# Moving the memsets of two V tiles behind the first scores, and three epsilon additions from GpSimd to VectorE, in a fused attention and GLU kernel

## The chip, the cores and the metric

The kernel runs on one core of one Trainium2 chip. The metric is the device time of one execution in microseconds (us), lower is better. The profile gives a second length, the span: from the first to the last instruction in the trace. Time and span are not the same thing.

PE is TensorE, PEld its weight loads, DVE is VectorE, ACT is ScalarE, POOL is GpSimd.

## The reference

```python
x  = A_x                                   # [1, 2048, 512], bf16
xn = layernorm(x)                          # (x - mean) / sqrt(var + 1e-5)
# A: sliding-window attention, 32 heads of 16, window 256
q, k, v = split_heads(xn @ wqkv)
p  = softmax(where(mask, q @ k.T * 16**-0.5, -1e9))
A  = merge_heads(p @ v) @ wo
# B: bilinear GLU
B  = ((xn @ w_gate) * (xn @ w_up)) @ w_down    # 1792 hidden
return x + A + B
```

## The kernel before

The 2048 rows are 16 row tiles of 128, in four chunks of four. PE does the projections, the scores, the values and the GLU in one hand-made order. Before PE can start on real work, the four row tiles of the first chunk must be normalised: VectorE makes the statistics, an epsilon is added, GpSimd takes the power -0.5, VectorE applies it (`xn`), PE transposes `xn`, ScalarE copies the transpose, and PE projects V, then K and Q.

```python
def setup(self):
    ...
    for _ in range(38):                                   # warm-up of PE
        nc.tensor.matmul(wps[:], lhsT=ident[:], rhs=ident[:], start=True, stop=True)
    ...
    self.new_values()                                     # first V tile

def new_values(self):                                     # three memsets on GpSimd
    ...
    nc.gpsimd.memset(self.heads(V)[:, :, :, 16:18], 1.0)
    nc.gpsimd.memset(V[:, VW - 16:], 0.0)
    nc.gpsimd.memset(VS[:, SW - 16:], 0.0)

def norm_scale(self, t, n=4):
    ...
    (nc.gpsimd if t else nc.vector).tensor_scalar(out=ve[:], in0=mv[:, :, 1], scalar1=1e-5, ...)   # var + eps
    nc.gpsimd.tensor_tensor(out=rs[:], in0=ve[:], in1=self.mhalf[:, 0:n], op=ALU.pow)

def first_chunk(self):
    self.new_chunk(0)
    for b in range(2):
        self.norm_stats(b, 1)
        self.norm_scale(b, 1)
    for b in (0, 1, 2, 3):
        self.norm_apply(b)                                # xn of tile b, on VectorE
        if b < 2:
            self.norm_stats(b + 2, 1)
            self.norm_scale(b + 2, 1)
    self.norm_transpose(0, False)
    for b in range(4):
        if b < 3:
            self.norm_transpose(b + 1, False)             # PE, then a copy on ScalarE
        self.proj_v(b, engine="act")                      # PE, then a copy on ScalarE
    self.proj_qk(0, 0, 1, engine="dve")                   # "first K projection" below
    self.proj_qk(0, 0, 0, engine="act")
    self.swap_halves(0, self.nc.scalar)
    for _ in range(2):
        self.new_values()                                 # second and third V tile
    self.proj_qk(0, 1, 1, engine="dve")
```

The softmax here doesn't subtract the row's maximum and nothing guards it: scores larger than these inputs give would overflow.

Of the kernel before, what the change touches and what calls it, by code (L numbers as in the profile page):

```python
# [11 lines left out]
ALU = mybir.AluOpType  # L12
# [16 lines left out]
class Kernel:  # L29
# [133 lines left out]
    def norm_scale(self, t, n=4):  # L163

        nc = self.nc
        mv = self.stats[t][0]
        ve = self.small.tile([128, n], F32, tag="ve", name="ve")
        (nc.gpsimd if t else nc.vector).tensor_scalar(out=ve[:], in0=mv[:, :, 1], scalar1=1e-5, scalar2=None,
                                                      op0=ALU.add)
        rs = self.small.tile([128, n], F32, tag="rs", name="rs")  # L170
        nc.gpsimd.tensor_tensor(out=rs[:], in0=ve[:], in1=self.mhalf[:, 0:n], op=ALU.pow)
        for u in range(t, t + n):
            self.stats[u][2] = rs
# [75 lines left out]
# [7 lines that stand above are left out]
            self.norm_apply(b)  # L256
# [6 lines that stand above are left out]
                self.norm_transpose(b + 1, False)  # L263
            self.proj_v(b, engine="act")
        self.proj_qk(0, 0, 1, engine="dve")
        self.proj_qk(0, 0, 0, engine="act")
        self.swap_halves(0, self.nc.scalar)
        for _ in range(2):
            self.new_values()
        self.proj_qk(0, 1, 1, engine="dve")  # L270


# [247 lines left out]
    def run(self):  # L520
        self.xns, self.stats, self.sums = {}, {}, {}
        self.now, self.free = 0, dict(act=0, dve=0)
        self.setup()
        NCH, LAG = self.NCH, 2
        RESERVE = 36
        self.first_chunk()
        steps, self.first, self.last = [], {}, {}
        for T in range(NCH):
            for pieces in self.batches(T):
                for c, *_ in pieces:  # L530
                    self.first.setdefault((T, c), len(steps))
                    self.last[T, c] = len(steps)
                steps.append((T, pieces))
        due = {g: key for key, g in self.last.items()}
        self.beside = {}
        work = self.fillers()
        total = sum(w[0] for w in work) - RESERVE + SCORES * len(steps) + VALUES * (len(due) - 1)
        spent, n = 0, 0
        self.free = dict(act=0, dve=0)
        valued, ready = -1, -1  # L540

        def fill(upto, group):
            nonlocal spent, n
            while n < len(work):
                cost, f, before, after = work[n]
                if after is not None and after > valued:
                    break
                if spent + cost / 2 > upto and not any(
                        w[2] is not None and w[2] <= group for w in work[n:]):
                    break  # L550
                spent += cost
                self.now = spent
                f()
                n += 1

        def values(g):
            nonlocal spent
            if g not in due:
                return False
            spent += VALUES  # L560
            self.now = spent
            self.values(*due[g])
            return True

        def divide(g):
            nonlocal ready
            self.divide(*due[g])
            ready = g

        for g, s in enumerate(steps):  # L570
            fill(-1, g)
            valued = ready
            spent += SCORES
            self.now = spent
            self.scores(*s)
            upto = total * (g + 1) / len(steps)
            if values(g - LAG):
                fill(min(spent + 4, upto), g)
                divide(g - LAG)
            for _, f in self.beside.get(g, ()):  # L580
                f()
            if g < len(steps) - 1:
                fill(upto, g)
                self.mask_diag(*s)
        T = NCH - 1
        self.ps_s.__exit__(None, None, None)
        late = self.ctx.enter_context(self.tc.tile_pool(name="ps_late", bufs=1, space=bass.MemoryType.PSUM))
        self.late = [late.tile([128, 512], F32, tag=f"L{i}", name=f"L{i}") for i in range(4)]
        fill(spent + 10, -1)
        self.mask_diag(*steps[-1])  # L590
        fill(spent + 10, -1)
        self.values(*due[len(steps) - 1], self.late)
        spent += VALUES
        divide(len(steps) - 1)
        valued = ready
        fill(spent + 15, -1)
        for b in range(3):
            self.wo(T, b, (3,))
            self.store(T, b)
        fill(10 ** 9, -1)  # L600
        assert n == len(work)
        self.wo(T, 3, (0, 1, 2, 3))
        self.store(T, 3, 0)
        self.store(T, 3, 1, True)
# [37 lines left out]
```

## Time and profile before

| | before |
|---|---|
| time, median | 267.34 us (267.24 to 268.01) |
| span of the profiled execution | 265.6 us |
| PE busy | 257.5 us, 97% |
| first K projection on PE | 11.12 us |

The page of the kernel before: its length, the busy time of each engine, and by engine the chain of work that ended last.

```profile
span 265.6 us, 8876 instructions
...
PE 257.5 (97%) x3860; PEld 119.0 (45%) x3881; DVE 176.1 (66%) x339; ACT 176.4 (66%) x143; POOL 114.6 (43%) x278
...
PE 94%; DVE 2%; issue 1%; DMA 1%; POOL 0%
```

PE is the limit nearly everywhere. The exception is the head, the first 11 us. Here is the timeline of the head of the kernel before. The columns are start (us), duration (us), engine, line, operation, output and inputs, shape, and in brackets the idle time of the engine before it and what ended it.

```profile
3.64 0.18 DVE L159 BATCH_NORM_AGGREGATE mv<-st 128x2 f32<-128x6 f32 x1
3.86 0.15 DVE L168 TENSOR_SCALAR ve<-mv 128x1 f32<-128x1 f32 x1
3.93 0.69 DVE L158 BATCH_NORM_STATS2 st<-x 128x6 f32<-128x512 bf16 x1
...
5.77 0.18 DVE L159 BATCH_NORM_AGGREGATE mv<-st 128x2 f32<-128x6 f32 x1
5.91 0.41 DVE L179 TENSOR_SCALAR xn<-x,mv,rs 128x512 bf16<-128x512 bf16 x1
...
6.37 0.40 PE L198 MATMUL xTp<-ident,xn 128*128 128x128 bf16 x4 [0.29 <-DVE xn L179]
...
7.08 0.41 DVE L179 TENSOR_SCALAR xn<-x,mv,rs 128x512 bf16<-128x512 bf16 x1
7.22 0.35 POOL L168 TENSOR_SCALAR ve<-mv 128x1 f32<-128x1 f32 x1 [0.18 <-DVE mv L159]
7.55 0.40 PE L198 MATMUL xTp<-ident,xn 128*128 128x128 bf16 x4
...
8.18 0.33 POOL L127 MEMSET V<- 128x256 bf16 x1
...
8.27 0.83 DVE L179 TENSOR_SCALAR xn<-x,mv,rs 128x512 bf16<-128x512 bf16 x1 [0.77 <-POOL rs L171]
...
8.85 0.60 ACT L218 ACTIVATE V<-vp 128x512 bf16<-128x512 f32 x1
9.16 0.40 PE L198 MATMUL xTp<-ident,xn 128*128 128x128 bf16 x4 [0.34 <-DVE xn L179]
...
9.59 0.60 ACT L199 ACTIVATE xnT<-xTp 128x512 bf16<-128x512 bf16 x1
...
11.12 2.54 PE L239 MATMUL qkp<-xnT,Wqkv 128*128 128x512 bf16 x11
```

Three things are to be seen. The last `xn` (8.27 us) takes 0.83 us while GpSimd does memsets; the others take 0.38 to 0.41. PE waits for that `xn` before the last four transposes (9.16 us). And an epsilon addition costs VectorE little by itself: it starts 0.22 us after the aggregate of its tile, and the next instruction follows 0.07 us later (3.64, 3.86, 3.93).

### The profile page before, as it was taken

To read this page: it belongs to the slowest core of one execution; us is meant where nothing else is said; L and a number is where in the kernel's file an instruction comes from. 1 tells how busy PE (TensorE), PEld (TensorE's weight loads), DVE (VectorE), ACT (ScalarE), POOL (GpSimd) and SP (SyncE) were. 2 spreads that over 40 slices of the span, in tenths; PEclk is the share of its full clock that TensorE was granted. 3 is DMA by queue.
4 is the path that set the end of the run, shared out by engine and by line. 5 is a ranking of instruction groups with operands and counts; after the bars stand their busy time and mean duration, and the time that the engine had idled before them with its cause. 6 is when DMAs were issued, how large, how long until landed. Compare 5 with 4: busy or idle time off the path is not lost.

```text
span 265.6 us, 8876 instructions
## 1 busy us (share of the span) xinstructions
PE 257.5 (97%) x3860; PEld 119.0 (45%) x3881; DVE 176.1 (66%) x339; ACT 176.4 (66%) x143; POOL 114.6 (43%) x278
## 2 busy tenths in 40 slices
PE   7999999999999999999999999999999999999994
PEld 7444444444444444444444444444444444444453
DVE  5477898787757667667765866766652676867152
ACT  3667687788556678687755667678866566767500
POOL 6324342426574535334585443435444353344500
PEclk9999999999999999999999999999999999999999
DMA  6999911120151000002022100000200010000002
GB/s 199 373 353 340 265 23 22 23 48 2 20 86 37 22 2 0 4 2 47 2 59 63 42 2 2 0 4 6 45 2 20 25 40 2 2 0 6 0 2 80
DMA packets 19351, 15.12 MB, mean 57 GB/s; under 512 B 7280, under 2 KB 19312, under 8 KB 19312
## 3 DMA queue, kind: packets, MB, share of 16 engines
q1 hardware_dynamic: 18624, 14.23, 18.8%
q8 instruction: 30, 0.49, 0.8%
q10 hardware_dynamic: 688, 0.33, 0.5%
q14 instruction: 9, 0.07, 0.1%
HBM read 9.70 MB, written 2.10 MB: 44 GB/s over the span
## 4 chain that ended last, share of the span: by engine, by line
PE 94%; DVE 2%; issue 1%; DMA 1%; POOL 0%
PE up L390 19%; PE gp L379 19%; PE psd L410 16%; PE qkp L239 11%; PE S L294 10%; PE acc L348 7%; PE psd L416 5%; PE vp L227 5%; PE L L410 2%; DVE st L158 1%; DMA x<-in_A_x_dram 1%; PE L L416 1%; DVE xn L179 1%; PE L L348 0%; DVE mv L159 0%
## 5 line engine op out<-in xcount | busy, mean ns | idle before, releaser
L301 ACT ACTIVATE P<-S 128x2048 bf16<-128x2048 f32 x75 | 140.7, 1876 | 47.4 <-PE S L294 39.2
L147 POOL TENSOR_SCALAR_AFFINE_SELECT P<-P 64x256 bf16<-64x256 bf16 x224 | 98.6, 440 | 128.9 <-ACT P L301 117.9
L390 PE MATMUL up<-xnT,Wu 128*128 128x512 bf16 x224 | 60.0, 380 | 0.0
L379 PE MATMUL gp<-xnT,Wg 128*128 128x512 bf16 x224 | 58.9, 380 | 0.0
L394 DVE TENSOR_TENSOR hT<-up,gsb 128x512 bf16<-128x512 f32 x56 | 38.5, 687 | 19.5 <-PE up L390 18.0
L410 PE MATMUL psd<-Wd,hT 128*128 128x512 bf16 (+1 forms) x195 | 48.9, 368 | 1.9 <-issue 1.8
L325 DVE TENSOR_TENSOR P<-P,diag 128x512 bf16<-128x512 bf16 (+1 forms) x75 | 29.9, 399 | 9.8 <-ACT P L301 9.8
L410 PEld LDWEIGHTS <-hT 128*128 128x128 bf16 x238 | 21.2, 98 | 25.0 <-issue 2.7
L354 DVE STREAM_TRANSPOSE at<-acc 128x512 f32<-128x512 f32 x30 | 19.7, 696 | 18.8 <-PE acc L348 18.8
L379 PEld LDWEIGHTS <-Wg 128*128 128x128 bf16 x224 | 20.7, 98 | 25.6 <-issue 1.9
L294 PE MATMUL S<-Q,K 16*64 16x320 bf16 (+4 forms) x720 | 30.9, 260 | 0.1
L390 PEld LDWEIGHTS <-Wu 128*128 128x128 bf16 x224 | 19.9, 98 | 25.0 <-issue 3.3
L294 PE MATMUL S<-Q,Ko 32*64 32x320 bf16 (+4 forms) x720 | 31.0, 260 | 0.0
L218 ACT ACTIVATE gsb<-gp 128x512 bf16<-128x512 f32 x34 | 20.0, 596 | 15.5 <-PE gp L379 13.5
L239 PE MATMUL qkp<-xnT,Wqkv 128*128 128x512 bf16 x128 | 30.0, 380 | 0.0
L294 PEld LDWEIGHTS <-K 16*64 16x64 bf16 x720 | 12.1, 103 | 31.8 <-issue 31.4
L348 PE MATMUL acc<-P,VS 64*32 64x320 bf16 (+4 forms) x672 | 18.7, 254 | 0.0
L348 PE MATMUL acc<-P,V 64*32 64x320 bf16 (+4 forms) x672 | 18.5, 254 | 0.0
L239 PEld LDWEIGHTS <-Wqkv 128*128 128x128 bf16 x128 | 11.7, 98 | 14.6 <-issue 1.6
L220 DVE CAST gsb<-gp 128x512 bf16<-128x512 f32 x22 | 15.2, 691 | 3.4 <-PE gp L379 2.0
L416 PE MATMUL psd<-Wo,OT 128*128 128x512 bf16 (+1 forms) x59 | 16.2, 369 | 0.2 <-issue 0.2
L348 PEld LDWEIGHTS <-V 64*32 64x32 bf16 x720 | 14.5, 90 | 3.2 <-issue 2.6
(56 smaller groups left out, 195.5 us busy)
## 6 DMA issues: line engine op xcount, KB each, us to landing
out_dram<-y SPq DMA_DIRECT2D x15, 128.0 KB, 1.7
Wg<-in_B_w_gate_dram SPq DMA_DIRECT2D x2, 896.0 KB, 10.9
Wu<-in_B_w_up_dram SPq DMA_DIRECT2D x2, 896.0 KB, 12.4
Wd<-in_B_w_down_dram SPq DMA_DIRECT2D x1, 1792.0 KB, 17.3
Wqkv<-in_A_wqkv_dram SPq DMA_DIRECT2D x3, 512.0 KB, 5.8
x<-in_A_x_dram SPq DMA_DIRECT2D x1, 1024.0 KB, 10.8
VS<-V SPq DMA_DIRECT2D x6, 144.0 KB, 2.8
x<-in_A_x_dram SPq DMA_DIRECT2D x1, 512.0 KB, 11.0
```

The costliest lines, as they stand in the source:

```text
L147: nc.gpsimd.affine_select(out=v, in_=v, pattern=pattern + [[1 if diag else -1, 64]], compare_op=ALU.is_ge if diag else ALU.is_gt, fill=0.0 ...
L218: nc.scalar.activation(out=out, in_=in_, func=ACT.Copy)
L239: nc.tensor.matmul(ps[:], lhsT=self.Wqkv[:, k, lo:lo + 128], rhs=self.xnT[T][:, :, k, :], start=(k == 0), stop=(k == 3))
L294: nc.tensor.matmul(S[64 * par:64 * par + 64, e, col:col + n], lhsT=(self.Ko if par else self.K)[U][rows, c, keys], rhs=self.Q[T][rows, c, ...
L301: nc.scalar.activation(out=P[:, :, 0:col], in_=S[:, :, 0:col], func=ACT.Exp, scale=0.25)
L325: self.nc.vector.tensor_tensor(out=v, in0=v, op=ALU.min, in1=self.diag.unsqueeze(1).unsqueeze(1).to_broadcast([128, 4, n, 64]))
L348: nc.tensor.matmul(accs[par][32 * e:32 * e + 32, q:q + n], lhsT=v, rhs=P[rows, e, col:col + n], start=(i == 0), stop=(i == len(todo) - 1), ...
L379: nc.tensor.matmul(ps[:], lhsT=self.Wg[:, k, 128 * f:128 * f + 128], rhs=self.xnT[T][:, :, k, :], start=(k == 0), stop=(k == 3))
L390: nc.tensor.matmul(ps[:], lhsT=self.Wu[:, k, 128 * f:128 * f + 128], rhs=self.xnT[T][:, :, k, :], start=(k == 0), stop=(k == 3))
L394: nc.vector.tensor_tensor(out=self.hT[T][:, f, :], in0=ps[:], in1=self.gsb[:], op=ALU.mult)
L410: nc.tensor.matmul(ps, lhsT=self.hT[T][:, f, 128 * b:128 * b + 128], rhs=self.Wd[:, f, c0:c1], start=(f == 0), stop=False)
L416: self.nc.tensor.matmul(ps, lhsT=self.OT[T][:, c, 128 * b:128 * b + 128], rhs=self.Wo[:, c, c0:c1], start=False, stop=(c == 3))
```

## The change

The intent: get the memsets of the second and third V tile out of the way of the last `xn`, and save the first chunk's norms a hand-over from VectorE to GpSimd by adding epsilon where the variance is made.

```diff
@@ norm_scale
-        (nc.gpsimd if t else nc.vector).tensor_scalar(out=ve[:], in0=mv[:, :, 1], scalar1=1e-5, scalar2=None,
-                                                      op0=ALU.add)
+        (nc.vector if t < 4 else nc.gpsimd).tensor_scalar(out=ve[:], in0=mv[:, :, 1], scalar1=1e-5, scalar2=None,
+                                                          op0=ALU.add)
@@ first_chunk
         self.swap_halves(0, self.nc.scalar)
-        for _ in range(2):
-            self.new_values()
         self.proj_qk(0, 1, 1, engine="dve")
@@ run, in the loop over score groups g
             self.scores(*s)
             upto = total * (g + 1) / len(steps)
+            if g in (1, 2):
+                self.new_values()
             if values(g - LAG):
```

## The prediction

> **What bounds the kernel.** TensorE: the page has PE busy 257.5 of 265.6 us (97%) at clock 0.998; the chain of waits is 94% PE. Only in the head, before PE runs without gaps at about 11 us, is something else the limit: the norms of the first chunk's four row tiles, a loop between VectorE and GpSimd. The change acts there. The most it could win is what PE waits there for xn of tiles 1, 2 and 3: 0.29, some 0.25 and 0.34 us (timeline and waits).
>
> **Removed.** (a) Six GpSimd memsets, 8.18 to 8.96 us, beside which the last xn took 0.83 us on VectorE; its siblings took 0.38 to 0.41. The Trainium skill, "SBUF — State Buffer", section "Who interferes with whom", says that VectorE in a two-port mode and GpSimd exclude each other for a whole instruction; the trace agrees. (b) Three epsilon additions on GpSimd (0.29, 0.36, 0.35 us).
>
> **Added.** Three epsilon additions on VectorE. Tile 0 already has one: it starts 0.22 us after its aggregate, the next instruction 0.07 later. Without one, the next instruction follows the aggregate after 0.10 to 0.14. So each adds 0.15 to 0.19 us to VectorE, which is in order and has no slack (its xn waited at most 0.05 us for tiles 1 and 2); the addition for tile b+1 stands in front of xn of tile b.
>
> **The sum (us, before to after).**
> - xn 0: 4.75 to 4.94, hidden: PE warms up until 5.34.
> - xn 1: 5.91 to 6.24; transposes 1 from 6.37 to 6.70.
> - xn 2: 7.08 to 7.58; transposes 2 from 7.55 to 8.04, second V projection from 7.79 to 8.28.
> - xn 3: 8.27 to 8.35..8.55, now 0.41 long, ending at 8.8..8.95, not 9.10. But PE is in the second V projection until 9.14, so transposes 3 go from 9.16 to 9.14: nothing won.
> - ScalarE is in order: the copy of the second V projection (8.85 to 9.34) stands before the copy of transposes 3 (9.59; copies follow at 0.49 at best, so 9.83). The fourth V projection needs it: 10.25 to 10.48. First K projection: 11.12 to 11.35.
>
> What the last tile wins, the second and third lose; the head ends level to 0.3 us later, my estimate 0.15 to 0.2.
>
> **Moved.** The memsets come after the masks of the second and third score groups, about 20.6 and 24.7 us. GpSimd idles 2.2 us before the third group; V1 is not needed before about 50 us. The later ones delay the epsilon and power of the next chunk's first tile (24.74) by 0.5 us, towards its xn at 26.20; VectorE has 0.43 us idle soon after. No PE cost expected. PE is dense to the end, so a shift of the head passes on one to one.
>
> **Time.** 267.45 us, 8 in 10 between 266.9 and 267.95; the spread of before (267.24 to 268.01) exceeds the effect. Faster by over 2%: 1%; within: 98%; slower: 1%.
>
> **Would show it right:** last xn near 0.41 us; xn 1 and 2 start 0.3 and 0.5 us later; transposes 3 wait for PE, not xn; their copy follows directly on the copy of V; first K projection at 11.2 to 11.4; memsets at 20 to 25 us without a PE gap. **Wrong:** first K projection before 11.0, or transposes 1 and 2 unmoved.
>
> **What would make it wrong.** VectorE may take the short addition in a gap that it has anyway: the head then wins up to 0.3 us. The powers on GpSimd, now starting during an xn, may be held until it ends; if xn 3 comes after 9.1, the head loses more. A memset that blocks VectorE at 25 us could open a PE gap.

## The result, and the profile after

| | before | changed |
|---|---|---|
| time, median of 6 | 267.35 us (267.24 to 268.01) | 267.91 us (267.87 to 269.46) |
| ratio, with 95% interval | | 1.0027 (1.0004 to 1.0051) |

A ratio is the mean time of one kernel's runs over that of the other's of the same rounds, so not quite the ratio of the medians. Five executions of the changed kernel lie between 267.87 and 268.03 us; one took 269.46 us, and that one left the profile. The median lies just inside the predicted range (top 267.95 us); the mean, 268.18 us, lies outside; and the change of the median, 0.56 us, is some five times the 0.11 us that the predicted 267.45 us meant.

The page of the changed kernel, from the 269.46 us execution:

```profile
span 267.4 us, 8874 instructions
...
PE 259.1 (97%) x3860; PEld 119.9 (45%) x3881; DVE 176.2 (66%) x342; ACT 176.3 (66%) x143; POOL 113.8 (43%) x275
```

Since that execution is not typical, I ran the same file again (`after_again` below). Its trace, of 267.86 us with a span of 265.8 us, answers to the head shown before. The same timeline of the typical execution:

```profile
4.59 0.18 DVE L159 BATCH_NORM_AGGREGATE mv<-st 128x2 f32<-128x6 f32 x1
4.80 0.15 DVE L168 TENSOR_SCALAR ve<-mv 128x1 f32<-128x1 f32 x1
4.88 0.40 DVE L179 TENSOR_SCALAR xn<-x,mv,rs 128x512 bf16<-128x512 bf16 x1
...
5.92 0.18 DVE L159 BATCH_NORM_AGGREGATE mv<-st 128x2 f32<-128x6 f32 x1
6.13 0.15 DVE L168 TENSOR_SCALAR ve<-mv 128x1 f32<-128x1 f32 x1
6.21 0.41 DVE L179 TENSOR_SCALAR xn<-x,mv,rs 128x512 bf16<-128x512 bf16 x1
...
6.67 0.40 PE L198 MATMUL xTp<-ident,xn 128*128 128x128 bf16 x4 [0.77 <-DVE xn L179]
...
7.16 1.02 PE L227 MATMUL vp<-Wqkv,xnT 128*128 128x512 bf16 x4
...
7.46 0.15 DVE L168 TENSOR_SCALAR ve<-mv 128x1 f32<-128x1 f32 x1
7.54 0.40 DVE L179 TENSOR_SCALAR xn<-x,mv,rs 128x512 bf16<-128x512 bf16 x1
...
8.02 0.39 PE L198 MATMUL xTp<-ident,xn 128*128 128x128 bf16 x4
...
8.38 0.41 DVE L179 TENSOR_SCALAR xn<-x,mv,rs 128x512 bf16<-128x512 bf16 x1 [0.44 <-POOL rs L171]
...
9.10 0.39 PE L198 MATMUL xTp<-ident,xn 128*128 128x128 bf16 x4
9.30 0.60 ACT L218 ACTIVATE V<-vp 128x512 bf16<-128x512 f32 x1
...
9.79 0.59 ACT L199 ACTIVATE xnT<-xTp 128x512 bf16<-128x512 bf16 x1
...
11.32 2.32 PE L239 MATMUL qkp<-xnT,Wqkv 128*128 128x512 bf16 x10
```

The last `xn` is down to 0.41 us, as intended, and no longer waited for by PE. But `xn` of tiles 1 and 2 start 0.30 and 0.46 us later than before (6.21 and 7.54 against 5.91 and 7.08), because each waits behind epsilon additions that VectorE did not have: two by tile 1, three by tile 2. The first K projection is 0.20 us later (11.32 against 11.12). The moved memsets, in the same trace:

```profile
20.83 0.33 POOL L127 MEMSET V<- 128x256 bf16 x1
...
24.87 0.33 POOL L127 MEMSET V<- 128x256 bf16 x1
```

The slow execution has the same VectorE times (its `xn` start at 5.01, 6.34, 7.67 and 8.51 us; x landed some 0.14 us later than in the typical trace). What differs is PE. The PE lines of its timeline:

```profile
6.80 0.61 PE L198 MATMUL xTp<-ident,xn 128*128 128x128 bf16 x4 [0.72 <-DVE xn L179]
7.20 1.49 PE L227 MATMUL vp<-Wqkv,xnT 128*128 128x512 bf16 x3
...
8.91 0.63 PE L198 MATMUL xTp<-ident,xn 128*128 128x128 bf16 x4 [0.22 <-issue]
...
10.72 0.39 PE L198 MATMUL xTp<-ident,xn 128*128 128x128 bf16 x4
...
12.93 0.59 PE L239 MATMUL qkp<-xnT,Wqkv 128*128 128x512 bf16 x2
```

Three V matmuls (of four; one record is missing) take 1.49 us here, four take 1.02 us in the typical trace. A single one of these matmuls is listed with 0.63 us in the slow trace and 0.38 us in the typical one, so they follow each other at (1.49 - 0.63) / 2 = 0.43 us instead of (1.02 - 0.38) / 3 = 0.21 us: PE ran at half its rate there, until about 10.4 us. The granted clock on the page doesn't show it (it reads 9 in all 40 slices of both traces), because its record begins only when full rate is first granted. That moment can be read from the record: 6.37 us after the start of the span in the trace of before, 5.58 us in the typical trace, 10.37 us in the slow one.

So there are two things to explain: why the typical execution is 0.5 us longer when its span is only 0.2 us longer (265.6 to 265.8), and why some executions lose 1.6 us more (I call these the slow ones).

### The profile page after: what moved, and what is told of

Same layout as the page of the kernel before. It is cut to its first block, busy times and chain, and to the rows that moved or that the text cites. A ratio compares the mean times of both kernels' runs of the same rounds, so it can differ in the third digit from the quotient of the medians.

```text
span 267.4 us, 8874 instructions
## 1 busy us (share of the span) xinstructions
PE 259.1 (97%) x3860; PEld 119.9 (45%) x3881; DVE 176.2 (66%) x342; ACT 176.3 (66%) x143; POOL 113.8 (43%) x275
## 4 chain that ended last, share of the span: by engine, by line
PE 95%; DVE 2%; issue 1%; DMA 1%; ACT 0%
PE up L388 19%; PE gp L377 19%; PE psd L408 16%; PE qkp L239 11%; PE S L292 10%; PE acc L346 7%; PE vp L227 5%; PE psd L414 5%; PE L L408 2%; DMA x<-in_A_x_dram 1%; DVE st L158 1%; PE L L414 1%; PE L L346 0%; PE xTp L198 0%; DVE xn L179 0%
## 5 line engine op out<-in xcount | busy, mean ns | idle before, releaser
L239 PEld LDWEIGHTS <-Wqkv 128*128 128x128 bf16 x128 | 11.7, 98 | 14.6 <-issue 1.6
L227 PE MATMUL vp<-Wqkv,xnT 128*128 128x512 bf16 x60 | 16.3, 403 | 0.2
## 6 DMA issues: line engine op xcount, KB each, us to landing
x<-in_A_x_dram SPq DMA_DIRECT2D x1, 1024.0 KB, 11.7
```

The source lines that it names most:

```text
L227: nc.tensor.matmul(ps[:], lhsT=self.xnT[T][:, b, k, :], rhs=self.Wqkv[:, k, 1024:1536], start=(k == 0), stop=(k == 3))
L239: nc.tensor.matmul(ps[:], lhsT=self.Wqkv[:, k, lo:lo + 128], rhs=self.xnT[T][:, :, k, :], start=(k == 0), stop=(k == 3))
```

## The experiments

All with five rounds, each call on one chip with the kernel before beside it. The median of before was 267.37, 267.34 and 267.34 us, with no execution above 267.47.

### First call: which half of the change, and is it PE's rate?

My first theory (G) was that PE's half rate explains all of it, more of it in one execution and less in another. The rival (V) was that only VectorE's order counts.

**after_again**: no edit.

> The changed kernel again, for a second trace. Theory G (PE rate): the longer PE wait before the transposes of tile 1 (0.72 us instead of 0.29) leaves PE at half rate, one 512-column matmul per 0.43 us instead of 0.216, for longer; how long varies between executions. Then the times spread: about 267.9 us, some near 269.5; a trace of a 267.9 us execution shows fewer or no half-rate V projections, and the first K projection near 11.7 instead of 12.93 us. Theory V (VectorE order alone): every execution pays 0.2 us, the 269.46 us one was an outlier for some other reason.

Measured: 267.86 us median, five executions from 267.85 to 267.97; ratio 1.0020 (1.0006 to 1.0034). No execution near 269.5. The typical loss is stable at 0.5 us, and its trace shows PE at full rate from 5.58 us. First K projection at 11.32, not 11.7. Theory G fails as the cause of the typical loss.

**memset_only**: the memsets alone.

```diff
-        (nc.vector if t < 4 else nc.gpsimd).tensor_scalar(   # as changed
+        (nc.gpsimd if t else nc.vector).tensor_scalar(       # as before
```

> Memsets moved, epsilons of tiles 1 to 3 back on GpSimd. V and G alike: xn 1 and xn 2 start at 5.91 and 7.08 as before, the last xn starts near 8.27 and takes 0.41 us instead of 0.83, first K projection at about 10.85 instead of 11.12, time 267.1 us (0.25 less than before). Theory M (the moved memsets cost time at 22 to 27 us, or where their tiles lie does): 267.5 us or more although the head is shorter.

Measured: 267.15 us median (267.10 to 267.50), 0.22 below before. The last `xn` in its timeline:

```profile
8.28 0.41 DVE L179 TENSOR_SCALAR xn<-x,mv,rs 128x512 bf16<-128x512 bf16 x1 [0.76 <-POOL rs L171]
...
8.83 0.39 PE L198 MATMUL xTp<-ident,xn 128*128 128x128 bf16 x4
...
11.05 2.54 PE L239 MATMUL qkp<-xnT,Wqkv 128*128 128x512 bf16 x11
```

So the memsets do what they were moved for, and no cost shows where they went: in this execution the span is 0.07 us shorter than in the trace of before (265.51 against 265.58), and the first K projection 0.07 us earlier. At 11.05 it came later than the 10.85 expected; in this execution full rate was granted only at 6.96 us, so its first transposes of tile 1 ran at half rate.

**eps_only**: the epsilons alone.

```diff
-        (nc.gpsimd if t else nc.vector).tensor_scalar(
+        (nc.vector if t < 4 else nc.gpsimd).tensor_scalar(   # memsets stay in first_chunk
```

> Epsilons on VectorE, memsets left in place. V: transposes 1 near 6.75, transposes 2 near 8.1, last xn 0.83 us again and ending near 9.35, first K projection 11.3 to 11.5, time 267.6. G: the PE wait before transposes 1 is the same 0.72 us as in the changed kernel, so half-rate matmuls as there: 267.9 to 268.2 us with some executions near 269.5.

Measured: 267.92 us median (267.84 to 267.98), none near 269.5. Its timeline has the early delay and the slow last `xn` together:

```profile
6.65 0.57 PE L198 MATMUL xTp<-ident,xn 128*128 128x128 bf16 x4 [0.58 <-DVE xn L179]
...
8.36 0.83 DVE L179 TENSOR_SCALAR xn<-x,mv,rs 128x512 bf16<-128x512 bf16 x1 [0.44 <-POOL rs L171]
```

The whole loss comes from the epsilons; with them on VectorE, moving the memsets is worth nothing (267.92 without, 267.86 with), since PE is then the limit at the last transposes.

**after_filled**: PE kept busy between the transposes of tiles 0 and 1.

```diff
         self.norm_transpose(0, False)
+        fps = self.s_tiles.tile([128, 4, 512], F32, tag="S", name="fps")
+        for _ in range(8):
+            self.nc.tensor.matmul(fps[:, 0, 0:128], lhsT=self.ident[:], rhs=self.ident[:], start=True, stop=True)
```

> The changed kernel with eight 128-column matmuls of the identity between the transposes of tile 0 and tile 1, so that PE doesn't idle there; VectorE, GpSimd and ScalarE unchanged. G: the V projections run at 0.216 us per matmul in every execution, first K projection at about 11.3 us, time 267.3 to 267.6 us, no execution near 269.5. V: nothing changes, 267.9 us.

Measured: 267.87 us median (267.79 to 268.11), as the changed kernel. A miss for G, and it agrees with `after_again`: idle PE is not what the typical execution pays for. (In its traced execution, the slowest of the five, the first V projection also waited 0.20 us for its weights to land.)

Put together, with the spans that each execution lists (to 0.1 us) beside its time; I call "time less span" the tail:

| | time, median | span, median | tail, mean |
|---|---|---|---|
| before (9 executions) | 267.37 | 265.6 | 1.73 |
| memsets moved | 267.15 | 265.4 | 1.72 |
| epsilons on VectorE | 267.92 | 265.8 | 2.07 |
| both (after_again) | 267.86 | 265.8 | 2.07 |

This table is the turning point. The span moves by 0.2 us, as the head does. The other 0.3 us (1.73 to 2.07) is outside the span, in the tail, and it goes with the epsilons.

### Second call: what lengthens the tail?

Theory C: the tail goes with how many instructions VectorE has. The VectorE rows in the traces, waits included, are 437 before, 437 with the memsets moved, and 439 in both kernels with the epsilons on VectorE. Rival: it comes with the later head or with GpSimd's fewer instructions.

**before_v3**: the kernel before with three idle-time VectorE instructions.

```diff
+        spare = const.tile([128, 1], F32, name="spare")
+        for _ in range(3):
+            nc.vector.memset(spare[:], 0.0)
         self.mhalf = const.tile([128, 4], F32, name="mhalf")
```

> The kernel before with three more VectorE instructions of one column each in its setup, where VectorE waits for x anyway; nothing else. The runs so far left 0.3 us of the 0.5 outside the span: time less span is 1.77 us before, 1.73 with the memsets alone moved, 2.07 and 2.08 with the epsilons on VectorE. Theory C (it goes with the number of VectorE instructions of the program): span 265.6, time less span about 2.07, time 267.65 us. Rival (it comes from the three fewer GpSimd instructions, or from the head being later): span 265.6 and time 267.35, as before.

Measured: 267.75 us median, span 265.7, tail 2.08 with 440 VectorE rows. The head didn't move (first K projection 11.06 us) and GpSimd is untouched. The tail came without a later head and without a change on GpSimd: theory C holds, the rival falls.

**after_vless**: the changed kernel with three setup instructions taken off VectorE.

```diff
-        nc.vector.memset(warm[:], 0.0)
+        nc.gpsimd.memset(warm[:], 0.0)                       # after the identity is made
-        nc.vector.tensor_scalar(out=podd[:], in0=pi[:], ...)
-        nc.vector.tensor_copy(out=self.odd[:], in_=podd[:])
+        self.parity()          # the same mask by six small GpSimd instructions after the norms
```

A first form of this kernel, with the bit operations simply given to GpSimd, was refused by the build (that engine has no such operations).

> The changed kernel with three setup instructions of VectorE (a memset and the two that make the odd mask) made on GpSimd instead, so that VectorE has as many instructions as before. Theory C: span 265.8 as the changed kernel, time less span back at 1.75, time 267.55 us. Rival (head later, or which engine adds epsilon): time less span 2.07 and 267.87 us.

Measured: 267.52 us median, span 265.8, tail 1.72 with 437 rows. The tail is back although the head is as late as in the changed kernel. One of its six executions took 269.20 us; it is the profiled one, with full rate granted at 10.69 us, a second slow trace of the same kind as the first. (Its span and tail, 267.5 and 1.7 us, show that the slow executions lose their time inside the span.)

**after_v1dve**: tests the prediction's ScalarE step.

```diff
-            self.proj_v(b, engine="act")
+            self.proj_v(b, engine="dve" if b == 1 else "act")
```

> The changed kernel with the copy of the second V projection on VectorE instead of ScalarE. The prediction had said that the ScalarE queue (this copy ahead of the copy of transposes 3) holds the fourth V projection by 0.23 us. If so: the copy of transposes 3 starts near 9.5 instead of 9.79 us, first K projection near 11.08 instead of 11.32, span 265.55, time 267.6 (tail 2.07 kept). Rival (PE or xn is the limit, the ScalarE order hides behind it): first K projection at 11.3, span 265.8, time 267.85.

Measured: 267.74 us median (267.68 to 267.83), span 265.7, tail 2.06. It is 0.40 us above before, the changed kernel 0.49 (267.86 less 267.37): about 0.1 us won, less than half of the 0.25 expected. In its timeline the copy of transposes 3 no longer stands behind a V copy:

```profile
9.43 0.69 DVE L220 CAST V<-vp 128x512 bf16<-128x512 f32 x1 [0.61 <-PE vp L227]
...
9.65 0.60 ACT L199 ACTIVATE xnT<-xTp 128x512 bf16<-128x512 bf16 x1 [0.16 <-PE xTp L198]
```

So taking the copy off ScalarE gained something, but less than expected. What ScalarE's order alone costs is not shown, since the edit also gives VectorE a copy of 0.69 us. The traced execution is the slowest of the five, with full rate only from 7.46 us, so its first K projection (11.29) can't be compared closely.

**memset_v1dve**: the same edit on top of memset_only.

> The memsets moved, the epsilons on GpSimd as before, the copy of the second V projection on VectorE: a candidate that beats both. First K projection near 10.87 instead of 11.05, span 265.35, time 267.0 us; if one more VectorE instruction is enough to lengthen the tail, 267.3.

Measured: 267.23 us median (267.13 to 267.67), span 265.3, tail 1.93 with 438 rows. The span is the shortest so far, and one VectorE instruction more took 0.2 us of it back in the tail. In all five executions the tail lies between 1.89 and 1.97, so 438 rows cost a little over half of what 439 cost (0.20 against 0.34 us).

### Third call: a step or a slope, and is PE's idle time what makes the slow executions?

**before_v12**: as before_v3, `range(12)`.

> As before_v3, with twelve more one-column VectorE instructions instead of three. So far time less span was 1.73 us with 437 VectorE instructions in the trace, 1.93 with 438, 2.07 with 439 and 440. If the tail is a step at one place of VectorE's instruction stream: span 265.6, tail 2.0 to 2.1, time 267.7. If each VectorE instruction costs about 0.1 us at the end: tail near 2.9, time 268.5.

Measured: 267.72 us, all five executions between 267.72 and 267.73; but span 266.0 and tail 1.72 with 449 rows. The time is what the step expected (267.7), but neither expectation had this span and tail; it is the most telling result. The head explains part of the span: twelve memsets took 1.4 us, longer than VectorE was free, so the first K projection came at 11.31 instead of 11.12. The rest is at the very end. These are rows of the traces that the busy views leave out, VectorE's last semaphore and drain instructions:

```
                before              before_v3           before_v12
semaphore       265.035 us          264.926 us          265.179 us
drain           265.146 us          265.036 us          265.646 us
from the first
to the second   0.111 us            0.110 us            0.467 us
```

In before_v12 VectorE stands still for 0.36 us more between two instructions that follow each other directly, in front of the 448th of its 449 rows. The other engines' drains are done by 265.49 us; GpSimd's last wait, for all engines, is released at 265.82, after VectorE's drain (265.39 before). So one pause at one place of VectorE's instruction stream fits the runs: with 435 to 437 rows its cost does not show, with 439 and 440 the place would lie beyond the last instruction of the trace and the pause would show as a longer tail, with 449 it lies inside the span. Part of it overlaps the other engines' last drains, so the span grows by 0.4 us and not by the full 0.19 + 0.36. This is read from one trace, the pauses of the other kernels would lie outside theirs, and the half cost at 438 rows stays unexplained. A fixed price per instruction is ruled out in any case: 439 and 440 rows cost the same, and 449 no more. The trace of before_v12 also has an 8192-byte packet of instructions at 266.3 us, after the span, which the traces of before and before_v3 don't have.

**memset_vless**: memset_only with the three setup instructions off VectorE.

> The memsets moved, epsilons on GpSimd, and three fewer VectorE instructions than before (warm memset and odd mask on GpSimd). Step: tail 1.7, time 267.15 as with the memsets alone. Per instruction: tail 1.4, time 266.85.

Measured: 266.96 us median (266.92 to 267.13), ratio 0.9987 (0.9974 to 0.9999), tail 1.74 with 435 rows. No fall of the tail below 1.7: again not a cost per instruction. The span is 265.2, 0.2 less than with the memsets alone; I did not look for the reason.

**candidate**: memset_vless with the copy of the second V projection on VectorE.

> The best of the pieces: memsets moved, epsilons on GpSimd, copy of the second V projection on VectorE, warm memset and odd mask on GpSimd so that VectorE has two instructions fewer than before. Span 265.3 (median), tail 1.73, time 267.05 us, 0.3 below before and 0.8 below the changed kernel.

Measured: 266.88 us median (266.80 to 267.14), ratio to before 0.9984 (0.9972 to 0.9997), tail 1.74 with 436 rows. It is below both kernels, by 0.46 us and, against the changed kernel's 267.86 of another call, by 0.98 us; both differences are well under 1%.

**after_short_warm**: the changed kernel with a shorter warm-up of PE.

```diff
-        for _ in range(38):
+        for _ in range(22):
```

> The changed kernel with 22 instead of 38 warm-up matmuls, so that PE idles from about 3.8 to 5.4 us as well as before transposes 1. If idle PE in the stretch before about 7 us is what kept the two slow traces (269.46 and 269.2 us) at 0.43 us per 512-column matmul until 10.6 us, most executions now do so: first K projection near 13 us, span about 267.4, time 269.4 us. If those two were outliers of another cause: 267.9 us.

Measured: 269.37 us median (269.23 to 269.94): all five executions are slow. PE in its timeline:

```profile
5.33 0.61 PE L198 MATMUL xTp<-ident,xn 128*128 128x128 bf16 x4 [1.39 <-DVE xn L179]
6.66 0.61 PE L198 MATMUL xTp<-ident,xn 128*128 128x128 bf16 x4 [0.72 <-DVE xn L179]
7.06 1.91 PE L227 MATMUL vp<-Wqkv,xnT 128*128 128x512 bf16 x4
...
10.51 0.39 PE L198 MATMUL xTp<-ident,xn 128*128 128x128 bf16 x4
```

More idle PE ahead of about 7 us makes the rare state the rule, with the same signature: half rate, 0.61 us for four transposes, until full rate is granted at 10.09 us. The Trainium skill, "TensorE: Matmul & The Clock Gate", section "What's actually happening", says that PE gets its full rate after a sufficiently busy window of about 3.4 us, and that the windows run freely and don't start with the kernel. The grant came at 4.05 to 7.46 us in the typical traces and at 10.09 to 10.69 us in the slow ones.

The packed traces agree, and show the windows themselves. The recorded stretch of full rate lasts 256.00, 259.41 or 262.83 us in all 14 traces, which is 75, 76 or 77 times 3.413 us, and it begins at another point of such a grid in nearly every trace. If a grant comes at the end of a window, one can go back from it by one window and add up PE's busy time in it (matmul rows; one trace of each kernel):

| trace | window, us | PE busy in it, us | full rate at its end |
|---|---|---|---|
| memset_only | 3.55 to 6.97 | 3.10 | yes |
| changed kernel (after_again, 267.86 us) | 2.17 to 5.58 | 3.41 | yes |
| eps_only | 3.63 to 7.04 | 2.84 | yes |
| after_v1dve | 4.05 to 7.46 | 2.80 | yes |
| after_vless (269.20 us) | 3.86 to 7.28 | 2.70 | no, at 10.69 |
| changed kernel (269.46 us) | 3.55 to 6.96 | 2.69 | no, at 10.37 |
| after_short_warm | 3.26 to 6.67 | 1.30 | no, at 10.09 |

In memset_only and in the slow trace of the changed kernel the window lies in the same place. The busy time differs by 0.41 us, which is the difference of PE's waits before transposes 1 (0.32 and 0.72). So, on this pair of traces, the longer wait cost the execution its window; in after_again, the same kernel, the window fell earlier and held no wait. Where the window falls decides which executions pay. In the table 2.80 us were enough and 2.70 were not, but that is no exact limit: memset_vless got full rate after a window with 2.64 us of warm-up matmuls. How often the changed kernel pays is not shown either. Of the 27 executions of the changed kernel, eps_only, after_vless and after_v1dve, which have the longer wait and the full warm-up, two were slow. Of the others with the full warm-up none lost as much; one execution of before took 268.01 us, and no trace of it was kept.

## Why the prediction was right or wrong, point by point

- **PE bounds the kernel, and the change acts in the head alone.** Right.
- **Removing the memsets frees the last `xn`.** Right: 0.83 to 0.41 us. Alone it is worth 0.22 us (memset_only).
- **Each epsilon adds 0.15 to 0.19 us to VectorE, in front of an `xn`.** Right: `xn` 1 at 6.21 (predicted 6.24), `xn` 2 at 7.54 (7.58), though x landed 0.06 us earlier than in the trace of before. The hand-over that was saved lay behind VectorE's own work for tiles 1 and 2, so saving it won nothing there.
- **The last tile wins nothing because PE is busy until 9.14.** Right: transposes 3 started at 9.10 and waited for no `xn`.
- **ScalarE's order then holds the fourth V projection.** Right in kind (copies at 9.30 and 9.79, predicted 9.34 and 9.83). Taking the copy off ScalarE won about 0.1 us (after_v1dve), so that its full 0.23 us could be won back is not shown.
- **First K projection at 11.35.** Right: 11.32 in the typical trace. In the slow one it is 12.93.
- **The moved memsets cost nothing.** Right: they ran at 20.83 and 24.87 us in the typical trace, and in the trace of memset_only span and head are shorter by the same 0.07 us.
- **"PE is dense to the end, so a shift of the head passes on one to one", and the time from it.** This step failed. It holds for the span, 265.6 to 265.8 us. But the sum took the time to move with the span, and left out a term: the tail grew from 1.73 to 2.07 us with the added VectorE instructions. Taking three instructions off VectorE removed exactly this (after_vless), adding three to the kernel before brought it (before_v3). That VectorE pauses at one place of its stream, as the 0.36 us in before_v12 suggest, is the likely reason, not a shown one. The point, 267.45, was also lower than its own sum: 267.34 plus the 0.23 us of the head is 267.57.
- **Not foreseen: the half-rate executions.** The prediction counted the longer wait of PE before transposes 1 only as the shift that it passes on. That wait is 0.72 us instead of 0.29, both with PE at half rate; the 0.77 of the typical trace is longer because PE, at full rate by then, was done earlier with transposes 0. It never asked what idle time does to PE's own rate. One execution of six lost 1.6 us so: its window had 2.69 us of PE work, and full rate came 3.41 us later than in memset_only. That put the mean outside the range.

What stays open: why VectorE pauses at that place of its stream (an instruction fetch is my guess, since the extra packet belongs to an instruction queue, but the packet comes after the pause and no run shows what VectorE waits for), why 438 rows cost half, and the exact limit of PE's busy time: 2.80 us of 3.41 was enough and 2.70 was not, but 2.64 was enough in memset_vless.

## What to carry to other kernels

An instruction moved to an engine "with time to spare" stands in a queue: ask what comes directly behind it there, and whether the hand-over it saves was the last thing waited for. When time and span differ by more or less than they did before, look outside the span, and test with dummy instructions in idle time; here 0.34 us came with three more instructions on one engine, whatever they did. In a head that warms PE up, idle PE can cost twice, as here: the wait, and the risk of running the next 3.4 us at half rate.

## What the Trainium skill lacked or had wrong

- "Runtime: NRT & Kernel Launch", section "Instruction fetch mechanics", calls the cost of crossing a block of instructions mostly hidden. The one fetch stall that it names is that of a taken branch, and none of the VectorE rows that the trace of before_v12 keeps is a branch. It has nothing on a pause near the end of a program: here VectorE lost 0.36 us in front of row 448 of its trace, and kernels with 439 or 440 rows had a tail of 2.06 to 2.08 us against 1.72 to 1.74 with 435 to 437, and 1.93 with 438. Whether a block boundary is the cause is not shown.
- "TensorE: Matmul & The Clock Gate", section "What's actually happening", describes the windows; no page says that less than a microsecond of idle PE during the warm-up can be enough to miss one. Here 0.72 us before transposes 1, 2.69 and 2.70 us busy in the window, went with grants at 10.37 and 10.69 us in two traces, one window after 6.96 and 7.28. The section also speaks of at least one busy window of 3.4 us; in memset_vless the grant came at 4.05 us, 2.6 us after the first warm-up matmul (1.41 us), so less than a whole window was enough.
- The same page, section "Part 4: PE-mode transpose", says that full rate doesn't engage for transposes. Once granted, it did here: four transposes took 0.40 us, against 0.61 us at half rate. The section adds that transposes don't count as busy in the same way; in the window of eps_only they were about 0.8 of the 2.84 us that were enough, while 2.63 us of warm-up matmuls alone were not (0.63 to 4.05 us in after_v1dve).
- "SBUF — State Buffer", section "Who interferes with whom", was right and useful: the `xn` of 0.41 us took 0.83 us beside GpSimd memsets (before, eps_only), and not once they were gone (memset_only, after_again). That one engine is locked out for a whole instruction is not seen by itself: the large memsets took 0.33 us beside the `xn` (8.18 us) and away from it (20.83 us).
